# Two layout changes of a fused attention and wave-MLP kernel, moved from TensorE to DMA transposes

## The chip, the core and the metric

The kernel runs on one core of a Trainium2 chip. The core has a matrix engine (TensorE, PE in the profile, with its weight loads shown apart as PEld), VectorE (DVE), ScalarE (ACT), GpSimd (POOL) and SyncE (SP). Matmul results land in PSUM; everything else lives in SBUF, and DMA queues move data between SBUF and device memory. Each engine works through its own list of instructions in order, and so does each DMA queue: a DMA that waits for its data holds back every DMA behind it on the same queue. The metric is the time of one execution on the device in microseconds; lower is better.

## The reference

First comes attention inside chunks of 64 tokens, for 8 batches of 576 tokens with 8 heads of 64. Its result x, with 512 channels per token, goes through one layer of a wave MLP with a residual:

```
scores = scale * q_c @ k_c^T          # per chunk of 64 tokens
x      = softmax(scores) @ v_c        # x: (8, 576, 512)
theta  = x @ w_theta
zr, zi = x * cos(theta), x * sin(theta)
y      = w_tok_r @ zr + w_tok_i @ zi  # mixes the 576 tokens of a batch
u      = x + y
out    = u + relu(u @ w_ch)
```

Inputs and outputs are float32; the kernel works in float16 with float32 sums.

## The kernel before, in words

The batches are taken in four pairs, numbered p = 0 to 3 in the code. A pair has 1152 tokens, that is nine tiles of 128 rows; tile 4 holds the last 64 tokens of the first batch and the first 64 of the second when outputs are written, and the last 64 tokens of both batches when attention is computed. The attention part treats the tiles in five groups: g = 0, 1, 3, 4 with two tiles each and g = 2 with the one mixed tile.

The steps, each a small function, are: a1 (PE transposes of q and k, then two copies out of PSUM), a2 (scores and exp), a3 (times v, then VectorE divides by the row sums and writes x with tokens on partitions), a4 (L341: PE transposes x, eight 128x128 blocks for a group of two tiles and four for the mixed one, and a copy moves the result to xT, channels on partitions), a5 (theta = x @ w_theta from xT, then cos and sin on ScalarE), z (the products; for the mixed tile two small DMAs on SP's queue put halves together in zm), y (L449: 18 matmuls per batch bb and channel block db; VectorE adds xT and writes uT, channels on partitions, at L463; yh is the same for the first batch of pair 0), w (L470) and st (out_tile, L491).

The function w does two things for a tile j of 128 tokens. For each of four channel blocks, uT is the stationary operand of a 512 wide matmul with w_ch (L475), which sums u @ w_ch, and then of a 128 wide matmul with the identity (L482), which puts u itself, tokens on partitions, into the other half of the same PSUM tile. ScalarE takes relu of the first half into SBUF (L488). In out_tile, VectorE adds the u half and the relu (L494), and SP's queue stores the tile (L496), in two DMAs for tile 4.

Nothing is scheduled at run time. The list ORDER is a written-out sequence of these steps (name, pair, group or block, and bits that choose the engine of a copy); the program emits them in this order, so each engine's own order follows from it. All PSUM tiles come from one pool of four buffers, two banks each, taken in turn; a step whose buffer is still being read waits. Of o, the output tile, there are four buffers; x has six, uT and xT two each. Loads of q, k and v with a cast to float16 go through POOL's queue. A DMA on SP's queue also waits for the one issued eight before it.

Of the kernel before, what the change touches and what calls it, by code (L numbers as in the profile page):

```python
# [9 lines left out]
FP32 = mybir.dt.float32  # L10
FP16 = mybir.dt.float16
AF = mybir.ActivationFunctionType
ALU = mybir.AluOpType
# [3 lines left out]


ORDER = """
a1.0.0:0 a2.0.0:0 a1.0.1:3 a3.0.0.0:0 a3.0.0.1:0 a2.0.1:0 a1.0.2:0 a3.0.1.0:0 a2.0.2:0  # L20
a3.0.2.0:0 a4.0.2:3 a4.0.0:0 a3.0.1.1:0 a5.0.2:0 a4.0.1:1 z.0.2.0:0 a5.0.1:0 a5.0.0:0
tw.1.2:0 z.0.0.0:0 z.0.0.1:0 tw.0.0:1 z.0.1.0:0 z.0.1.1:0 tw.1.1:1 tw.0.1:0 tw.0.2:0
tw.1.0:1 a1.0.3:2 yh.0.0:0 a2.0.3:0 yh.0.1:0 a1.0.4:2 a3.0.3.0:0 yh.1.0:0 a3.0.3.1:0
a2.0.4:0 yh.1.1:0 a1.1.0:0 a3.0.4.0:0 a3.0.4.1:0 w.0.0:0 a2.1.0:0 a4.0.3:0 st.0.0:0
a4.0.4:1 a3.1.0.0:0 a1.1.1:0 a3.1.0.1:0 a5.0.3:0 a4.1.0:1 w.0.1:0 st.0.1:0 a5.0.4:0
a1.1.2:2 z.0.3.0:0 a5.1.0:0 w.0.2:0 z.0.4.0:0 z.0.3.1:0 z.0.4.1:0 a2.1.1:0 st.0.2:0
a1.1.3:2 w.0.3:0 st.0.3:0 y.0.1.0:0 a2.1.2:0 a3.1.1.0:0 a1.1.4:1 a3.1.2.0:0 a2.1.3:0
y.0.1.1:0 a1.2.0:0 a3.1.3.0:0 a3.1.1.1:0 y.0.1.2:0 a2.1.4:0 a3.1.3.1:0 z.1.0.0:0
a1.2.1:3 a2.2.0:0 a3.1.4.0:0 y.0.1.3:0 a1.2.2:0 a3.1.4.1:0 a2.2.1:0 a4.1.1:1 z.1.0.1:0
w.0.4:0 st.0.4:0 a4.1.2:0 a4.1.3:0 w.0.5:0 st.0.5:0 a3.2.1.0:0 a1.2.3:2 a5.1.2:0 w.0.6:0  # L30
z.1.2.0:0 a5.1.1:0 st.0.6:0 w.0.7:0 a5.1.3:0 st.0.7:0 z.1.1.0:0 a4.1.4:1 w.0.8:0
st.0.8:0 a1.2.4:1 z.1.1.1:0 a3.2.1.1:0 a5.1.4:0 z.1.3.0:0 z.1.4.0:0 y.1.0.0:0 a2.2.2:0
z.1.4.1:0 a3.2.0.0:0 z.1.3.1:0 a1.3.0:3 y.1.0.1:0 y.1.1.0:0 a2.2.3:0 a3.2.0.1:0 a2.2.4:0
a1.3.1:3 a3.2.3.0:0 y.1.0.2:0 a1.3.2:0 a3.2.2.0:0 a2.3.0:0 a2.3.1:0 a1.3.3:0 a3.2.3.1:0
y.1.0.3:0 a4.2.0:0 a4.2.2:0 a4.2.1:0 y.1.1.1:0 a2.3.2:0 a3.3.0.0:0 a1.3.4:0 a3.2.4.0:0
a2.3.3:0 w.1.0:0 a5.2.2:0 a5.2.0:0 st.1.0:0 z.2.2.0:0 w.1.1:0 a4.2.3:1 a5.2.1:0 st.1.1:0
z.2.0.0:0 z.2.1.0:0 y.1.1.2:0 z.2.0.1:0 a3.2.4.1:0 a3.3.3.0:0 w.1.2:0 a5.2.3:0 st.1.2:0
z.2.1.1:0 y.1.1.3:0 a3.3.0.1:0 a3.3.1.0:0 w.1.3:0 st.1.3:0 y.2.0.0:0 a4.2.4:1 w.1.4:0
a3.3.2.0:0 st.1.4:0 a3.3.3.1:0 z.2.3.0:0 a5.2.4:0 y.2.0.1:0 a4.3.0:0 a4.3.2:1 z.2.3.1:0
w.1.5:0 st.1.5:0 z.2.4.0:0 y.2.0.2:0 a4.3.3:0 w.1.6:0 a2.3.4:0 st.1.6:0 a3.3.1.1:0  # L40
z.2.4.1:0 y.2.0.3:0 w.1.7:0 a4.3.1:1 st.1.7:0 y.2.1.0:0 a3.3.4.0:0 a3.3.4.1:0 a5.3.2:0
a5.3.1:0 z.3.1.0:0 w.1.8:0 a5.3.0:0 st.1.8:0 w.2.0:0 z.3.2.0:0 y.2.1.1:0 st.2.0:0
w.2.1:0 z.3.0.0:0 z.3.0.1:0 st.2.1:0 z.3.1.1:0 a5.3.3:0 y.2.1.2:0 w.2.2:0 a4.3.4:1
st.2.2:0 y.2.1.3:0 w.2.3:0 z.3.3.0:0 st.2.3:0 a5.3.4:0 w.2.4:0 z.3.3.1:0 y.3.0.0:0
w.2.5:0 z.3.4.0:0 st.2.4:0 st.2.5:0 y.3.0.1:0 w.2.6:0 st.2.6:0 y.3.0.2:0 z.3.4.1:0
w.2.7:0 st.2.7:0 y.3.0.3:0 w.2.8:0 y.3.1.0:0 w.3.0:0 st.2.8:0 y.3.1.1:0 w.3.1:0 st.3.0:0
st.3.1:0 y.3.1.2:0 w.3.2:0 st.3.2:0 y.3.1.3:0 w.3.3:0 st.3.3:0 w.3.4:0 st.3.4:0 w.3.5:0
w.3.6:0 st.3.5:0 st.3.6:0 w.3.7:0 st.3.7:0 w.3.8:0 st.3.8:0
""".split()


# [1 line left out]
def kernel(  # L53
# [11 lines left out]
    nc = tc.nc  # L65
    B, H, S, D = q.shape
    DM = H * D
    CH = 64
    P = 128
    NDB = DM // P  # L70
    NE = H // 2
    NP = B // 2
    T = 2 * S
    NT = T // P
    HS = S // 2
    KT = S // P
# [22 lines left out]
    id16 = const.tile([P, P], FP16, name="id16")  # L99
# [131 lines left out]
    st = {}  # L231
# [4 lines left out]
    def once(p, key, make):  # L236
        if key not in st[p]:
            st[p][key] = make()
        return st[p][key]
# [9 lines left out]
    def xT_tile(p):  # L249
        return once(p, "xT", lambda: pairp.tile([P, NDB, T], FP16, name="xT"))  # L250

    def uT_tile(p):
        return once(p, "uT", lambda: pairp.tile([P, NDB, T], FP16, name="uT"))
# [87 lines left out]
    def a4(p, g, bits):  # L341

        j0, n = GROUPS[g]
        ps = psum2("ps_xT", FP16)
        psv = ps[:, 0 : NDB * n * P].rearrange("p (a s) -> p a s", a=NDB)
        for jj in range(n):
            for db in range(NDB):
                nc.tensor.transpose(  # L348
                    psv[:, db, jj * P : jj * P + P],
                    st[p]["x", g][:, jj, db * P : db * P + P],  # L350
                    id16,
                )
        xT = xT_tile(p)
        if n == 2:
            copy(bits & 1, xT[:, :, x_col(j0) : x_col(j0) + n * P], psv)
            return
        xm = trig.tile([P, NDB, P], FP16, name="xTm", bufs=1)
        st[p]["xTm"] = xm
        copy(bits & 1, xm, psv)
        copy(  # L360
            not bits & 2,
            xT.rearrange("p a (b s) -> p a b s", b=2)[:, :, :, KT * P : S],
            xm.rearrange("p a (b s) -> p a b s", b=2),
        )

    def a5(p, g):
# [82 lines left out]
    def y(p, bb, db):  # L449
# [17 lines left out]
            op=ALU.add,  # L467
        )

    def w(p, j):  # L470

        uT = uT_tile(p)
        ps = psum2("ps_uw")
        for db in range(NDB):
            nc.tensor.matmul(  # L475
                ps[:, 0:DM],
                uT[:, db, j * P : j * P + P],
                wch16[:, db, :],
                start=(db == 0),
                stop=(db == NDB - 1),  # L480
            )
            nc.tensor.matmul(  # L482
                ps[:, DM + db * P : DM + db * P + P],
                uT[:, db, j * P : j * P + P],
                id16,
            )
        r = outp.tile([P, DM], FP32, name="relu", bufs=3)
        nc.scalar.activation(out=r, in_=ps[:, 0:DM], func=AF.Relu)  # L488
        st[p]["w", j] = (ps, r)

    def out_tile(p, j):  # L491
        ps, r = st[p].pop(("w", j))
        o = outp.tile([P, DM], FP32, name="o32")
        nc.vector.tensor_tensor(out=o, in0=ps[:, DM : 2 * DM], in1=r, op=ALU.add)  # L494
        for pp, bb, s0, n in out_ranges(j):
            nc.sync.dma_start(out[2 * p + bb, s0 : s0 + n, :], o[pp : pp + n])  # L496


    BATCH = [[0, 1, 2], [3, 4]]
# [2 lines left out]
    def load(i):  # L502
        load_qk(*LOADS[i])
        load_v(*LOADS[i])
# [13 lines left out]
    load_w(moe_w_ch, wch16)  # L518
    for i in range(5, NAT):
        load(i)  # L520
    loaded = NAT
    seen = set()
    emit = dict(a1=a1, a2=a2, a3=a3, a4=a4, a5=a5, z=z, y=y, yh=yh, w=w,
                st=out_tile, tw=tw)
    for item in ORDER:
        name, bits = item.split(":")
        kind, *args = name.split(".")
        args = [int(i) for i in args]
        if kind in ("a1", "a4", "tw"):
            emit[kind](*args, int(bits))  # L530
        else:
            emit[kind](*args)
        seen.add(name)

        while loaded < len(LOADS):
            p, g = LOADS[loaded]
            pn, gn = LOADS[loaded - NAT]
            need = {f"a1.{pn}.{gn}"}
            if p >= 2:
                need |= {f"a3.{p - 2}.{g}.{hg}" for hg in range(GROUPS[g][1])}  # L540
            if not need <= seen:
                break
            load(loaded)
            loaded += 1
# [29 lines left out]
```

The softmax here doesn't subtract the row's maximum and nothing guards it: scores larger than these inputs give would overflow.

## Time and profile before

| what | value |
|---|---|
| median of 11 runs (lowest to highest) | 223.03 us (221.8 to 224.67) |
| the profiled execution's own time | 224.2 us |
| its span from first to last instruction | 222.1 us |
| PE busy | 199.5 us (90%) |
| DVE, ACT, POOL busy | 130.9, 117.4, 85.1 us |
| mean granted TensorE clock | 0.992 |
| chain that ended last, PE's share | 82% |

Busy time of the engines in stretches of the span, from the trace: in 0 to 12 us PE works 3.73 us, in 12 to 35 us 16.98 of 23, in 60 to 85 us 22.29 of 25, in 85 to 110 us 25.00 of 25, in 110 to 135 us 24.49 of 25, and in 135 to 211 us it has no idle time. POOL's DMAs fill the first half of the span; in 110 to 222 us POOL has none. Times in the profile are microseconds, "mean ns" is the duration of one instruction, and because matmuls are pipelined, two matmuls that follow each other are closer together than one's duration.

### The profile page before, as it was taken

To read this page: it belongs to the slowest core of one execution; us is meant where nothing else is said; L and a number is where in the kernel's file an instruction comes from. 1 tells how busy PE (TensorE), PEld (TensorE's weight loads), DVE (VectorE), ACT (ScalarE), POOL (GpSimd) and SP (SyncE) were. 2 spreads that over 40 slices of the span, in tenths; PEclk is the share of its full clock that TensorE was granted. 3 is DMA by queue.
4 is the path that set the end of the run, shared out by engine and by line. 5 is a ranking of instruction groups with operands and counts; after the bars stand their busy time and mean duration, and the time that the engine had idled before them with its cause. 6 is when DMAs were issued, how large, how long until landed. Compare 5 with 4: busy or idle time off the path is not lost.

```text
span 222.1 us, 6717 instructions
## 1 busy us (share of the span) xinstructions
PE 199.5 (90%) x2994; PEld 139.5 (63%) x2994; DVE 130.9 (59%) x230; ACT 117.4 (53%) x136; POOL 85.1 (38%) x118
## 2 busy tenths in 40 slices
PE   0575889989999888999999999999999999999992
PEld 0464458767578665566787755667765676777751
DVE  0145556766585683768765539777665653653553
ACT  2243796046996355699247696416758425221242
POOL 7897488579796598848600000000000000000000
PEclk9999999999999996999999999999999999999999
DMA  6999999999999999999990012112211221321236
GB/s 60 176 125 188 195 183 182 175 151 140 171 198 221 127 143 172 196 205 238 172 77 6 3 47 74 47 50 47 99 47 49 88 79 50 94 94 49 96 117 215
DMA packets 83612, 26.92 MB, mean 121 GB/s; under 512 B 76288, under 2 KB 78976, under 8 KB 83584
## 3 DMA queue, kind: packets, MB, share of 16 engines
q0 software_dynamic: 77696, 16.54, 83.9%
q1 hardware_dynamic: 5888, 9.96, 13.2%
q8 instruction: 23, 0.38, 0.7%
q14 instruction: 5, 0.04, 0.1%
HBM read 33.06 MB, written 9.44 MB: 191 GB/s over the span
## 4 chain that ended last, share of the span: by engine, by line
PE 82%; ACT 7%; DVE 5%; issue 2%; DMA 2%; POOL 0%; ACTq 0%; POOLq 0%
PE ps_y L455 27%; PE ps_uw L475 14%; PE ps_theta L377 14%; PE ps_qkT L266 8%; PE ps_y L434 4%; PE ps_sT L292 4%; PE ps_xT L348 4%; PE ps_uw L482 4%; PE ps_x L320 3%; DMA qk<-in_k_dram 2%; ACT kT L199 2%; ACT eT L299 2%; DVE x L334 1%; DVE kT L197 1%; DVE qT L197 1%
## 5 line engine op out<-in xcount | busy, mean ns | idle before, releaser
L455 PE MATMUL ps_y<-wT,z 128*128 128x288 f16 x448 | 59.5, 286 | 0.0
L455 PEld LDWEIGHTS <-z 128*128 128x128 f16 x448 | 42.6, 98 | 12.9 <-issue 0.3
L176 POOL DMA_DIRECT2D v<-in_v_dram x56 | 42.0, 762 | 18.0 <-DMA qk<-in_k_dram 10.8
L475 PE MATMUL ps_uw<-wch,uT 128*128 128x512 f16 x144 | 43.5, 386 | 0.0
L488 ACT ACTIVATE relu<-ps_uw 128x512 f32<-128x512 f32 x36 | 21.5, 598 | 39.3 <-PE ps_uw L482 39.2
L463 DVE TENSOR_TENSOR uT<-ps_y,xT 128x576 f16<-128x576 f32 x28 | 21.2, 756 | 26.9 <-PE ps_y L455 26.8
L494 DVE TENSOR_TENSOR o<-ps_uw,relu 128x512 f32<-128x512 f32 x36 | 24.7, 689 | 19.2 <-ACT relu L488 19.1
L482 PE MATMUL ps_uw<-id,uT 128*128 128x128 f16 x144 | 31.9, 222 | 0.0
L377 PE MATMUL ps_theta<-wtheta,xT 128*128 128x512 f16 x128 | 30.1, 379 | 0.8 <-DVE xT L197 0.8
L299 ACT ACTIVATE eT<-ps_sT 128x1024 f16<-128x1024 f32 (+1 forms) x20 | 18.6, 940 | 20.7 <-PE ps_sT L292 20.7
L266 PE MATMUL ps_qkT<-id,qk 128*64 128x128 f16 (+1 forms) x640 | 22.3, 226 | 6.9 <-DMA qk<-in_q_dram 5.8
L387 ACT ACTIVATE cos<-ps_theta,pihalf 128x1024 f16<-128x1024 f32 (+1 forms) x20 | 20.6, 1031 | 11.4 <-PE ps_theta L377 11.3
L334 DVE TENSOR_TENSOR x<-ps_x,recip 128x512 f16<-128x512 f32 x36 | 24.9, 692 | 1.2
L266 PEld LDWEIGHTS <-qk 128*64 128x64 f16 (+1 forms) x640 | 19.1, 118 | 9.7 <-DMA qk<-in_q_dram 5.8
L475 PEld LDWEIGHTS <-uT 128*128 128x128 f16 x144 | 14.3, 99 | 15.3 <-issue 0.8
L199 ACT COPY kT<-ps_qkT 128x1024 f16<-128x1024 f16 (+1 forms) x11 | 12.6, 1149 | 20.6 <-DVE qT L197 20.5
L155 POOL DMA_DIRECT2D qk<-in_k_dram x24 | 19.1, 797 | 4.1 <-DMA qk<-in_q_dram 2.7
L377 PEld LDWEIGHTS <-xT 128*128 128x128 f16 x128 | 11.8, 98 | 14.0 <-DVE xT L197 1.0
L155 POOL DMA_DIRECT2D qk<-in_q_dram x24 | 19.3, 805 | 1.9 <-issue 1.0
L391 ACT ACTIVATE sin<-ps_theta 128x1024 f16<-128x1024 f32 (+1 forms) x20 | 18.7, 936 | 0.0
L292 PE MATMUL ps_sT<-qT,kT 64*64 64x64 f16 x576 | 13.0, 224 | 5.7 <-ACT kT L199 3.3
L197 DVE COPY kT<-ps_qkT 128x1024 f16<-128x1024 f16 (+1 forms) x9 | 11.1, 1235 | 7.3 <-ACT qT L199 7.3
(51 smaller groups left out, 207.5 us busy)
## 6 DMA issues: line engine op xcount, KB each, us to landing
out_dram<-o SPq DMA_DIRECT2D x32, 256.0 KB, 2.0
qk<-in_q_dram POOLq DMA_DIRECT2D x16, 256.0 KB, 6.4
qk<-in_k_dram POOLq DMA_DIRECT2D x16, 256.0 KB, 7.6
v<-in_v_dram POOLq DMA_DIRECT2D x40, 64.0 KB, 6.6
v<-in_v_dram POOLq DMA_DIRECT2D x16, 128.0 KB, 6.2
out_dram<-o SPq DMA_DIRECT2D x8, 128.0 KB, 2.4
wnat<-in_moe_w_tok_r_dram POOLq DMA_DIRECT2D x2, 288.0 KB, 8.1
wnat<-in_moe_w_tok_i_dram POOLq DMA_DIRECT2D x2, 288.0 KB, 9.5
```

The costliest lines, as they stand in the source:

```text
L155: nc.gpsimd.dma_start(t[(pp // 2) : (pp // 2) + m // 2, ti].rearrange("p h t d -> p h (t d)"), src.rearrange("h (p t) d -> p h (t d)", t=2),)
L176: nc.gpsimd.dma_start(v16[pp : pp + m, sl, :, 0:D], v[2 * p + bb, :, s0 : s0 + m, :].rearrange("h s d -> s h d"),)
L266: nc.tensor.transpose(psv[par * D : par * D + D, w, e, tk, 0:rows], t[0:rows, w, 2 * e + par, tk, :], id16[0:rows, 0:rows],)
L292: nc.tensor.matmul(psv[kh * CH : kh * CH + CH, par, i, e, :], kT[par * D : par * D + D, e, c0 : c0 + CH], qT[par * D : par * D + D, e, c0 ...
L299: nc.scalar.activation(out=eT[:, 0:n].rearrange("p i e r c -> p r (i e) c"), in_=psv[:, :, 0:n].rearrange("p r i e c -> p r (i e) c"), fun ...
L334: nc.vector.tensor_tensor(out=xo, in0=px[:, :, :, 0:D], in1=recip.broadcast_to((P, 2, NE, D)), op=ALU.mult,)
L377: nc.tensor.matmul(ps[:, jj * DM : jj * DM + DM], xt[:, db, :], wtheta16[:, db, :], start=(db == 0), stop=(db == NDB - 1),)
L455: nc.tensor.matmul(psv[:, hf, 0:HS], zt[:, db * P : db * P + P], wT[:, kt, hf * HS : hf * HS + HS], start=(kt == 0), stop=(kt == 2 * KT),)
L475: nc.tensor.matmul(ps[:, 0:DM], uT[:, db, j * P : j * P + P], wch16[:, db, :], start=(db == 0), stop=(db == NDB - 1),)
L482: nc.tensor.matmul(ps[:, DM + db * P : DM + db * P + P], uT[:, db, j * P : j * P + P], id16,)
L488: nc.scalar.activation(out=r, in_=ps[:, 0:DM], func=AF.Relu)
L494: nc.vector.tensor_tensor(out=o, in0=ps[:, DM : 2 * DM], in1=r, op=ALU.add)
```

## The change

For pair 0, u is still turned by PE and ends as before. For pairs 1 to 3 (U_DMA = 1) the identity matmuls and the relu go away. A new step ut issues a DMA transpose on SP's queue, which turns one channel block of uT, over 512 tokens (bb = 0) or 640 tokens (bb = 1), into the tile un with tokens on partitions: eight DMAs per pair. The end of a tile is then one VectorE instruction, max(u @ w_ch, 0) + u, which reads the matmul's result in PSUM and un in SBUF.

For pairs 2 and 3 (X_DMA = 2) the step a4 goes away. A new step xt turns x into xT by DMA transposes on SP's queue, one per tile of 128 tokens: nine DMAs per pair. The copy that spreads the mixed tile over xT becomes a step of its own, xm. Outputs of pairs 2 and 3 (ST_POOL = 2) are stored through POOL's queue, those of pairs 0 and 1 through SP's as before. ORDER is written anew as a whole.

The lines of the diff, with most of ORDER left out (its parts that matter are quoted in the prediction):

```diff
+    U_DMA = 1
+    X_DMA = 2
+    ST_POOL = 2
...
         copy(bits & 1, xm, psv)
+        xm_copy(p, bits >> 1)
+
+    def xt(p, g):
+        j0, n = GROUPS[g]
+        x = st[p]["x", g]
+        xT = xT_tile(p)
+        if n == 1:
+            xm = trig.tile([P, NDB, P], FP16, name="xTm", bufs=1)
+            st[p]["xTm"] = xm
+            nc.sync.dma_start_transpose(xm, x[:, 0, :])
+            return
+        for jj in range(n):
+            c0 = x_col(j0 + jj)
+            nc.sync.dma_start_transpose(xT[:, :, c0 : c0 + P], x[:, jj, :])
+
+    def xm_copy(p, bits):
         copy(
-            not bits & 2,
-            xT.rearrange("p a (b s) -> p a b s", b=2)[:, :, :, KT * P : S],
-            xm.rearrange("p a (b s) -> p a b s", b=2),
+            not bits & 1,
+            xT_tile(p).rearrange("p a (b s) -> p a b s", b=2)[:, :, :, KT * P : S],
+            st[p]["xTm"].rearrange("p a (b s) -> p a b s", b=2),
         )
...
+    def un_tile(p, bb):
+        return once(p, ("un", bb), lambda: pairp.tile(
+            [P, KT + bb, DM], FP16, name=f"un{bb}", bufs=1))
+
+    def ut(p, bb, db):
+        cols = slice(KT * P, T) if bb else slice(0, KT * P)
+        nc.sync.dma_start_transpose(
+            un_tile(p, bb)[:, :, db * P : db * P + P], uT_tile(p)[:, db, cols]
+        )
+
     def w(p, j):
...
-            nc.tensor.matmul(
-                ps[:, DM + db * P : DM + db * P + P],
-                uT[:, db, j * P : j * P + P],
-                id16,
-            )
-        r = outp.tile([P, DM], FP32, name="relu", bufs=3)
-        nc.scalar.activation(out=r, in_=ps[:, 0:DM], func=AF.Relu)
+            if p < U_DMA:
+                nc.tensor.matmul(
+                    ps[:, DM + db * P : DM + db * P + P],
+                    uT[:, db, j * P : j * P + P],
+                    id16,
+                )
+        r = None
+        if p < U_DMA:
+            r = outp.tile([P, DM], FP32, name="relu", bufs=3)
+            nc.scalar.activation(out=r, in_=ps[:, 0:DM], func=AF.Relu)
         st[p]["w", j] = (ps, r)
...
-        nc.vector.tensor_tensor(out=o, in0=ps[:, DM : 2 * DM], in1=r, op=ALU.add)
+        if p < U_DMA:
+            nc.vector.tensor_tensor(out=o, in0=ps[:, DM : 2 * DM], in1=r, op=ALU.add)
+        else:
+            nc.vector.scalar_tensor_tensor(
+                out=o,
+                in0=ps[:, 0:DM],
+                scalar=0.0,
+                in1=un_tile(p, int(j >= KT))[:, j % KT if j < KT else j - KT],
+                op0=ALU.max,
+                op1=ALU.add,
+            )
+        eng = nc.sync if p < ST_POOL else nc.gpsimd
         for pp, bb, s0, n in out_ranges(j):
-            nc.sync.dma_start(out[2 * p + bb, s0 : s0 + n, :], o[pp : pp + n])
+            eng.dma_start(out[2 * p + bb, s0 : s0 + n, :], o[pp : pp + n])
```

More of the change, by code (lines that the diff above doesn't have):

```diff
@@ L19 @@
 ORDER = """
[L20 to L48, printed above, removed]
+a1.0.0:3 a1.0.1:2 a2.0.0:0 a1.0.2:3 a2.0.2:0 a2.0.1:0 a3.0.0.0:0 a3.0.0.1:0 a3.0.2.0:0
+a3.0.1.0:0 a3.0.1.1:0 a4.0.2:0 a4.0.0:0 a4.0.1:1 a5.0.2:0 z.0.2.0:0 a5.0.0:0 z.0.0.0:0
@@ new lines @@
+a5.0.1:0 tw.1.2:0 tw.0.0:0 tw.1.1:1 z.0.1.0:0 z.0.0.1:0 tw.0.2:1 a1.0.3:0 z.0.1.1:0
+tw.0.1:0 tw.1.0:1 a2.0.3:0 yh.0.0:0 a1.0.4:2 a3.0.3.0:0 yh.0.1:0 a3.0.3.1:0 a2.0.4:0
+yh.1.0:0 a3.0.4.0:0 a1.1.0:3 a3.0.4.1:0 a2.1.0:0 a4.0.3:1 a4.0.4:0 a3.1.0.0:0 a5.0.3:0
+z.0.3.0:0 a3.1.0.1:0 a1.1.1:0 yh.1.1:0 z.0.3.1:0 a5.0.4:0 a1.1.2:2 z.0.4.0:0 z.0.4.1:0
+a2.1.1:0 a1.1.3:2 w.0.0:0 st.0.0:0 y.0.1.0:0 a2.1.2:0 a1.1.4:0 a2.1.3:0 a3.1.1.0:0
+y.0.1.1:0 a4.1.0:0 a3.1.1.1:0 a1.2.0:0 a3.1.2.0:0 a3.1.3.0:0 y.0.1.2:0 a4.1.1:0 a4.1.2:1
@@ new lines @@
+a2.1.4:0 a2.2.0:0 a3.1.3.1:0 w.0.1:0 st.0.1:0 a5.1.2:0 a4.1.3:1 a5.1.1:0 w.0.2:0
+z.1.2.0:0 a5.1.0:0 z.1.1.0:0 st.0.2:0 z.1.1.1:0 z.1.0.0:0 w.0.3:0 z.1.0.1:0 st.0.3:0
+y.0.1.3:0 a3.1.4.0:0 a1.2.1:3 a3.1.4.1:0 w.0.4:0 st.0.4:0 y.1.0.0:0 a4.1.4:1 a5.1.3:0
+a5.1.4:0 z.1.4.0:0 y.1.0.1:0 a3.2.0.0:0 z.1.3.0:0 a1.2.2:1 z.1.4.1:0 ut.1.0.0:0 a2.2.1:0
+a1.2.3:2 w.0.5:0 st.0.5:0 y.1.0.2:0 a2.2.2:0 a1.2.4:1 z.1.3.1:0 a3.2.0.1:0 ut.1.0.1:0
+a3.2.2.0:0 y.1.0.3:0 a3.2.1.0:0 a2.2.4:0 a2.2.3:0 a1.3.0:0 ut.1.0.2:0 xt.2.2:0
@@ new lines @@
+a3.2.4.0:0 a1.3.1:0 y.1.1.0:0 a1.3.2:1 a3.2.1.1:0 xm.2.2:0 xt.2.0:0 ut.1.1.0:0 a2.3.0:0
+y.1.1.1:0 a3.2.4.1:0 a3.2.3.0:0 w.0.6:0 xt.2.1:0 a5.2.2:0 a5.2.0:0 st.0.6:0 w.0.7:0
+z.2.2.0:0 a5.2.1:0 st.0.7:0 z.2.1.0:0 y.1.1.2:0 w.0.8:0 z.2.1.1:0 z.2.0.0:0 st.0.8:0
+ut.1.0.3:0 a3.3.0.0:0 z.2.0.1:0 a2.3.1:0 y.1.1.3:0 a1.3.3:1 a3.3.0.1:0 a3.2.3.1:0
+y.2.0.0:0 a2.3.2:0 xt.2.4:0 a3.3.1.0:0 a1.3.4:0 a3.3.1.1:0 xt.2.3:0 a2.3.3:0 ut.1.1.1:0
+y.2.0.1:0 a3.3.3.0:0 a2.3.4:0 a3.3.2.0:0 ut.1.1.3:0 a5.2.4:0 w.1.0:0 st.1.0:0 xt.3.0:0
@@ new lines @@
+ut.1.1.2:0 y.2.0.2:0 w.1.1:0 st.1.1:0 a5.2.3:0 w.1.2:0 st.1.2:0 xt.3.1:0 z.2.3.0:0
+z.2.3.1:0 a5.3.0:0 z.2.4.0:0 w.1.3:0 st.1.3:0 xt.3.2:0 ut.2.0.1:0 a3.3.4.0:0 y.2.0.3:0
+a3.3.4.1:0 z.2.4.1:0 a3.3.3.1:0 w.1.4:0 a5.3.1:0 w.1.5:0 ut.2.0.2:0 z.3.0.0:0 ut.2.0.3:0
+st.1.4:0 st.1.5:0 z.3.1.0:0 z.3.1.1:0 z.3.0.1:0 xt.3.3:0 y.2.1.0:0 w.1.6:0 xm.3.2:0
+a5.3.2:0 st.1.6:0 xt.3.4:0 y.2.1.1:0 w.1.7:0 z.3.2.0:0 y.2.1.2:0 w.1.8:0 ut.2.0.0:0
+st.1.7:0 y.2.1.3:0 st.1.8:0 w.2.0:0 y.3.0.0:0 st.2.0:0 w.2.1:0 a5.3.4:0 ut.2.1.0:0
@@ new lines @@
+ut.2.1.1:0 w.2.2:0 st.2.1:0 a5.3.3:0 st.2.2:0 ut.2.1.3:0 w.2.3:0 st.2.3:0 y.3.0.1:0
+z.3.4.0:0 z.3.4.1:0 ut.2.1.2:0 z.3.3.0:0 z.3.3.1:0 w.2.4:0 y.3.0.2:0 w.2.5:0 st.2.4:0
+ut.3.0.1:0 ut.3.0.2:0 y.3.0.3:0 st.2.5:0 w.2.6:0 st.2.6:0 y.3.1.0:0 w.2.7:0 st.2.7:0
+y.3.1.1:0 w.2.8:0 ut.3.0.0:0 ut.3.0.3:0 st.2.8:0 y.3.1.2:0 ut.3.1.0:0 w.3.0:0 ut.3.1.1:0
+st.3.0:0 ut.3.1.2:0 y.3.1.3:0 w.3.1:0 w.3.2:0 ut.3.1.3:0 st.3.1:0 st.3.2:0 w.3.3:0
+w.3.4:0 w.3.5:0 st.3.3:0 w.3.6:0 st.3.4:0 w.3.7:0 st.3.5:0 st.3.6:0 st.3.7:0 w.3.8:0
@@ L49 @@
+st.3.8:0
 """.split()
@@ L523 @@
     emit = dict(a1=a1, a2=a2, a3=a3, a4=a4, a5=a5, z=z, y=y, yh=yh, w=w,
-                st=out_tile, tw=tw)
+                st=out_tile, tw=tw, xt=xt, xm=lambda p, g, bits: xm_copy(p, bits), ut=ut)
     for item in ORDER:
@@ L528 @@
         args = [int(i) for i in args]
-        if kind in ("a1", "a4", "tw"):
+        if kind in ("a1", "a4", "tw", "xm"):
             emit[kind](*args, int(bits))
```

## The prediction

> **What bounds the kernel now.** I read the page's busy times first, then the slices of the span, then the chain that ended last.
>
> ```profile
> PE 199.5 (90%) x2994; PEld 139.5 (63%) x2994; DVE 130.9 (59%) x230; ACT 117.4 (53%) x136; POOL 85.1 (38%) x118
> ...
> PE   0575889989999888999999999999999999999992
> ...
> POOL 7897488579796598848600000000000000000000
> PEclk9999999999999996999999999999999999999999
> DMA  6999999999999999999990012112211221321236
> ...
> q0 software_dynamic: 77696, 16.54, 83.9%
> q1 hardware_dynamic: 5888, 9.96, 13.2%
> ...
> PE 82%; ACT 7%; DVE 5%; issue 2%; DMA 2%; POOL 0%; ACTq 0%; POOLq 0%
> ...
> L475 PE MATMUL ps_uw<-wch,uT 128*128 128x512 f16 x144 | 43.5, 386 | 0.0
> L488 ACT ACTIVATE relu<-ps_uw 128x512 f32<-128x512 f32 x36 | 21.5, 598 | 39.3 <-PE ps_uw L482 39.2
> ...
> L494 DVE TENSOR_TENSOR o<-ps_uw,relu 128x512 f32<-128x512 f32 x36 | 24.7, 689 | 19.2 <-ACT relu L488 19.1
> L482 PE MATMUL ps_uw<-id,uT 128*128 128x128 f16 x144 | 31.9, 222 | 0.0
> ...
> out_dram<-o SPq DMA_DIRECT2D x32, 256.0 KB, 2.0
> ...
> zm<-zmid SPq DMA_DIRECT2D x8, 64.0 KB, 3.9
> ```
>
> From about 85 us on PE has no gap, while loads and POOL end at half the span. VectorE and ScalarE wait for PE (39.2 and 19.1 us of relu and o idle are waits down PE's own output). So in the second half a PE microsecond is a real one, and the DMA engines are nearly free. All removed PE work lies there.
>
> What one matmul costs in the stream is read not from "mean ns" but from the chain in order of time:
>
> ```profile
> 86.12 0.43 PE ps_uw L475
> ...
> 145.83 0.45 PE ps_xT L348 x8
> ...
> 208.80 0.22 PE ps_uw L475
> 209.02 0.06 PE ps_uw L482
> 209.07 2.21 PE ps_y L455 x18
> 211.28 0.21 PE ps_uw L475
> ```
>
> From one 512 wide matmul to the next are 0.27 us, of which the identity matmul has 0.055. Eight x transposes take 0.45 us, 0.056 each. At 211.28 the last y is done; the span's last 10.8 us are the tail: uT's add, six tiles of w, relu, o, store.
>
> **The change part by part.**
>
> *PE.* Identity matmuls: 27 tiles x 4 x 0.055 = 5.9 us. Transposes of x: 2 pairs x 36 x 0.056 = 4.0 us. What counts is the end of the last y. Ahead of it go 4.0 us of x transposes and 19 tiles x 0.22 = 4.2 us (pair 1, pair 2, one tile of pair 3); and the new order has one w of pair 3 ahead of the last y where the old has three, which moves 2 x 1.09 = 2.2 us behind it. Sum **-10.4 us**.
>
> *ScalarE and VectorE.* 27 relus of 0.598 (16.1 us) go; so do ten copies of xT and xTm (0.69 on VectorE, 1.01 on ScalarE). The new end instruction reads PSUM and SBUF as L494 does; the trace has no row of it. Bounds: 0.42 (a 64-row product of 512) and 0.689 + 0.598, the two it replaces; I take 0.69, L494's. All lies beside PE: nothing, as long as PE is the bound. If not, ScalarE still has 16 us less.
>
> *The transposes.* 42 DMAs come onto SP's queue: 18 for x and 12 for u of 128 KB, 12 for u of 160 KB; some 20 stores leave it for POOL. The trace has no transpose. Cheapest price: the hardware queue's own rate, 9.96 MB in 13.2% of 222.1 us, so 0.39 us for 128 KB. Dearest: if pieces of 64 bytes count like the software queue's packets (83.9% x 222.1 x 16 / 77696 = 38.4 ns on one engine), 2048 / 16 x 38.4 = 4.9 us. I take pieces of 256 bytes, a row of one 128 block, since those loads average 213 bytes a packet: 512 / 16 x 38.4 ns = **1.23 us** for 128 KB, 1.54 for 160. Landing after that: 2.0 us as the stores; zm's 3.9 is the other end, partly under the loads. With these prices the queue works 30 x 1.23 + 12 x 1.54 = 55 us plus about 11 for zm and stores, in some 110 us.
>
> *A wait.* SP's queue is in order, and stores now stand before transposes. The tightest place: the store of tile 1.0 waits for its o, behind it stand both transposes of xt.3.0, and PE needs them at a5.3.0. From the end of w.1.0 PE has y 2.21, w 0.87, a5 1.73, w 0.87 = 5.7 us; the path is o 0.69, store issue 0.34, 2 x 1.23, landing 2.0, with 0.1 of hand-overs 5.6. An o that finds VectorE inside another 0.69 operation is late by that: **+0.6**. At a5.3.1 PE has 6.5 us for the same path.
>
> *The tail.* After the last y: uT add 0.76; transpose 1.54 + 2.0; o of tile 4 0.69, at 5.0. Its two stores are on POOL, 0.77 each (POOL's rows for loads) where SP's take 0.34. The fifth o needs the buffer of tile 4, whose stores have landed at 5.0 + 1.54 + 2.0 to 3.1 (POOL's fastest landing seen for a load) = 8.5 to 9.6; then 0.69, 0.77, landing, and the 0.6 us close of now: 12.6 to 14.8, I take 13.7 against 10.8, **+2.9**.
>
> *The start.* The new order puts two groups' q, k transposes before the first scores and takes group 2 before group 1. Group 2's q and k land near 12.0 us (issued 7.2, median landing 4.8), then come 32 transposes 0.6, drain 0.2, copies 0.59 and 0.73, and both groups' scores 0.37 and 0.62: the first a3 has its turn near 15.1 us, where it now starts with the landing of v at 14.1. By 28 us both orders meet the landing of the token weights (issue 17.7 and 18.4, landing 9.5). I take **+1.0**; bounds -3 (the 1.8 us stall at 82.4 and the half clock behind it, shown by the 0.43 us line above, do not come back) and +3.
>
> Sum: -10.4 + 0.6 + 2.9 + 1.0 = -5.9; span 222.1 to 216.2. The profiled execution took 224.2, 1.2 over the median of 223.03; the median stands 0.9 over this span. So **217.1 us**.
>
> [...]
>
> **The rivals.**
>
> *SP's queue becomes the bound (slower).* From the end of w.0.8 to z.3.2 PE has 37.3 us of work, and SP must issue 20 transposes (20.75 units of 128 KB), eight stores (2.7 us) and two zm (1.1). It keeps up to 33.5 / 20.75 = 1.6 us per unit. Beyond, each 0.1 us costs 2.1 us in this stretch alone, up to 4.5 if no later slack takes it up (45 units in all). At 2.0 us: +8 to +18 on 217.1, so 225 to 235; at 2.5 at least 236. The 5.9 us gained are gone 0.13 to 0.28 us past 1.6, near 1.8. For it: a transpose must cut rows up, and 256 byte pieces are my choice; smaller ones reach the point at once. Against: SP is idle now, and the DMA share is one to three tenths.
>
> *Landing is late, not the queue.* With zm's 3.9 instead of 2.0, a5.3.0 is late by 1.9, a5.3.1 by 1.2, the tail by 1.9: +5, about 222. For it: the median of the only small SBUF to SBUF move; against: half of those fell into the loads.
>
> *Transfers are hidden anyway.* At 0.39 us the tail shortens by 1 and the 0.6 goes; with the start's gain of 3 instead of its loss, 217.1 - 5 = about 212; without, 215.5.
>
> **How the numbers follow.** Chances: forecast 0.45 (own range 214.5 to 220.5, the bounds of start and tail), hidden 0.12, late landing 0.10, queue bound 0.33 (half of it under 232). Half a per cent, 1.1 us, is what this measurement can tell. Late landing lies on the line: 0.03 of it faster, 0.04 same, 0.03 slower. Faster gets 0.45 + 0.12 + 0.03, less 0.02 for the forecast's upper end, 0.58; same 0.04 and 0.03 from both sides, 0.07; slower 0.35. The range 213.5 to 232 leaves out about 0.03 below and 0.16 above.
>
> **What would show it.** PE's group L482 has 36 matmuls instead of 144 and the x transposes 72; from 110 us PE's slices stay at 9. If the queue bounds, PE's waits name xT (a5.2, a5.3) or zm of pair 3, SP's queue waits for no one, and the clock falls in stalls as at 86 us. Transposes longer than 1.6 us apart on SP would make me wrong; so would a tail over 15 us, or the first 85 us changed by over 3.

## The result, and the profile after

| | before | after |
|---|---|---|
| median (lowest to highest) | 223.15 us (221.51 to 228.11, 47 executions) | 220.32 us (218.68 to 222.75, 12 executions) |
| ratio, after to before | | 0.9867, 95% interval 0.9835 to 0.9899 |
| profiled execution: its time, its span | 224.2, 222.1 us | 220.16, 218.0 us |
| end of the last y | 211.28 us | 204.36 us |
| from there to the end of the span | 10.8 us | 13.6 us |

The change makes the kernel 1.3% faster, about half of the 2.7% forecast; 220.32 lies inside the range given. Where a kernel's own executions spread by more than 1.5% (u alone, and the change's second run after2, below), its ratio is made from its lowest few, and I use the median of all there.

The page of the changed kernel, busy times, slices, queues, shares of the chain, and two groups:

```profile
PE 191.5 (88%) x2814; PEld 130.1 (60%) x2814; DVE 126.9 (58%) x223; ACT 98.8 (45%) x106; POOL 96.0 (44%) x138
...
PE   0666978969999999999957999999999999999970
...
PEclk9999999997999999999988999999999999999997
DMA  5999999999999999999999923463668568283883
...
q1 hardware_dynamic: 27648, 11.15, 26.9%
q8 instruction: 22, 0.36, 0.7%
...
PE 72%; DMA 12%; POOL 4%; issue 4%; ACT 4%; DVE 2%; POOLq 0%; DVEq 0%; ACTq 0%
...
L537 DVE SCALAR_TENSOR_TENSOR o<-ps_uw,un 128x512 f32<-128x512 f32 x27 | 18.3, 688 | 9.5 <-PE ps_uw L512 7.0
```

PE has lost 180 matmuls and is still the engine that sets the pace. Three things are new: the slices 57 in PE's row near 109 to 120 us, where it had nines; clock digits below 9 at 49 to 55 us and at 109 to 120 us, where before had a single 6, at 83 to 89 us; and "issue" with 4% of the chain, where before it had 2%. The end instruction takes 688 ns, VectorE and ScalarE stay far from their limits.

The transposes themselves, from the views of the tiles un and xT (columns: shortest/median/longest ns of one on SP's queue, first and last start in us), and from the list of DMA issues (last column: median us from issue to landing):

```profile
L503 SPq DMA_TRANSPOSE un<-uT x24: 1189/1272/2635, 91.8 to 205.2; - x24
```

```profile
L383 SPq DMA_TRANSPOSE xT<-x x16: 1200/1257/2277, 107.6 to 170.2; - x16
```

```profile
un<-uT SPq DMA_TRANSPOSE x24, 3.0
xT<-x SPq DMA_TRANSPOSE x16, 3.1
xTm<-x SPq DMA_TRANSPOSE x2, 6.4
```

So a transpose holds the queue for 1.26 us, and lands 3.0 us after the beginning of its issue, that is about 1.5 us after it lets go of the queue. The two mixed tiles, one of them issued among the last loads, have a median of 6.4; the six transposes issued between 91 and 111 us, while loads still ran, took 8.0 to 11.2 us to land.

Where the time up to the last y went is read by stages. The rows below are the windows of the two kernels, before first; the columns are window, width, then busy us (count) of PE, PE's weight loads, VectorE, ScalarE and POOL, then granted clock, DMA share (packets that overlap are each counted, so it can pass 1) and GB/s.

```profile
0.00:12.00 12.00, 3.73 (x82) 3.17 (x84) 0.87 (x3) 3.41 (x3) 10.12 (x19) 1.00 1.29 121
40.00:62.00 22.00, 21.26 (x400) 13.86 (x398) 15.01 (x28) 12.88 (x14) 16.53 (x23) 1.00 1.79 158
62.00:100.00 38.00, 35.28 (x708) 25.32 (x700) 25.59 (x45) 24.51 (x29) 28.30 (x39) 0.96 1.83 181
100.00:135.00 35.00, 34.49 (x667) 25.40 (x666) 22.36 (x41) 24.56 (x28) 8.53 (x11) 1.00 0.77 90
```

```profile
0.00:12.00 12.00, 4.86 (x102) 3.97 (x104) 2.04 (x4) 2.30 (x2) 10.36 (x20) 1.00 1.30 121
40.00:62.00 22.00, 19.64 (x386) 13.41 (x384) 13.88 (x27) 11.81 (x11) 17.19 (x25) 0.92 1.87 154
62.00:100.00 38.00, 38.00 (x655) 27.12 (x653) 26.95 (x49) 25.64 (x31) 27.57 (x38) 1.00 1.87 182
100.00:135.00 35.00, 30.72 (x549) 21.47 (x548) 19.97 (x38) 20.80 (x24) 8.59 (x11) 0.95 1.28 113
```

Width less PE's busy time is its idle time: 8.27, 0.74, 2.72 and 0.51 us before, 7.14, 2.36, 0.00 and 4.28 after (12 to 40 us is alike, 6.0 in both, and from 135 us to the last y there is none): 18.3 against 19.8 us, +1.5. The other loss is half clock, a stretch in which the clock records of the trace have the granted clock at 0.5: a matmul of L475 took 0.43 us of the chain of before in it (at 86.12 us) and 0.22 outside (at 208.80). Up to the last y there is one such stretch of 3.41 us before (from 85.5 us) and there are two after (from 48.4 and 113.2 us); PE has no idle time in them, so I put the cost of each at half its length, 1.7 us, and the difference at +1.7. The windows show them as 0.96, 0.92 and 0.95. The stops of 62 to 100 us have gone; in the chain of before they were

```profile
72.86 0.90 issue
...
82.44 1.81 issue
```

New ones have come ahead of them and behind them. The end of the last y moved by -6.9 us, from 211.28 to 204.36; without the +1.5 and the +1.7 that is -10.1 us for the matmuls that went.

The chain of the changed kernel in order of time shows the new stalls:

```profile
47.50 0.69 PE ps_sT L301 x32
...
50.18 2.65 PE ps_theta L403 x8
...
107.67 0.95 PE ps_qkT L275 x29
108.62 3.12 issue
111.74 0.30 PE ps_qkT L275 x3
...
113.30 3.96 PE ps_y L481 x18
...
118.01 0.18 PE ps_sT L301 x6
118.19 1.16 issue
119.35 0.56 PE ps_sT L301 x23
```

PE stops for 3.12 us in the middle of the 32 transposes of one step, waiting for nothing that the profile shows, and the y behind it takes 3.96 us instead of 2.21. It stops again at 118 us. The stall at 45 us is another: PE waits 2.18 us for kT (k transposed, which the scores need), and then runs eight theta matmuls in 2.65 us instead of 1.73. In the list of waits (total us, times, longest) it is the longer of these two:

```profile
PE ps_sT L301 <- DVE kT L206: 3.7, 2, 2.2
```

### The profile page after: what moved, and what is told of

Same layout as the page of the kernel before. It is cut to its first block, busy times and chain, and to the rows that moved or that the text cites. A ratio compares the mean times of both kernels' runs of the same rounds, so it can differ in the third digit from the quotient of the medians.

```text
span 218.0 us, 6379 instructions
## 1 busy us (share of the span) xinstructions
PE 191.5 (88%) x2814; PEld 130.1 (60%) x2814; DVE 126.9 (58%) x223; ACT 98.8 (45%) x106; POOL 96.0 (44%) x138
## 4 chain that ended last, share of the span: by engine, by line
PE 72%; DMA 12%; POOL 4%; issue 4%; ACT 4%; DVE 2%; POOLq 0%; DVEq 0%; ACTq 0%
PE ps_y L481 30%; PE ps_theta L403 12%; PE ps_uw L512 12%; DMA qk<-in_k_dram 7%; PE ps_qkT L275 6%; PE ps_sT L301 4%; DMA wtheta<-in_moe_w_theta_dram 3%; PE ps_y L460 3%; PE ps_x L329 3%; PE ps_xT L357 2%; POOL v L185 2%; DMA un<-uT 1%; ACT kT L208 1%; POOL out_dram L547 1%; POOL qk L164 1%
## 5 line engine op out<-in xcount | busy, mean ns | idle before, releaser
L481 PE MATMUL ps_y<-wT,z 128*128 128x288 f16 x448 | 61.2, 291 | 0.0
L481 PEld LDWEIGHTS <-z 128*128 128x128 f16 x448 | 43.7, 100 | 15.2
L547 POOL DMA_DIRECT2D out_dram<-o x20 | 10.9, 546 | 90.0 <-DVE o L537 90.0
L512 PE MATMUL ps_uw<-wch,uT 128*128 128x512 f16 x144 | 37.4, 379 | 0.2 <-ACT sin L417 0.2
L403 PE MATMUL ps_theta<-wtheta,xT 128*128 128x512 f16 x128 | 31.2, 391 | 0.0
L537 DVE SCALAR_TENSOR_TENSOR o<-ps_uw,un 128x512 f32<-128x512 f32 x27 | 18.3, 688 | 9.5 <-PE ps_uw L512 7.0
L403 PEld LDWEIGHTS <-xT 128*128 128x128 f16 x128 | 12.6, 101 | 15.2 <-issue 2.2
L208 ACT COPY kT<-ps_qkT 128x1024 f16<-128x1024 f16 (+1 forms) x11 | 13.3, 1205 | 10.5 <-DVE qT L206 10.3
L428 DVE TENSOR_TENSOR z<-x,cos 128x1024 f16<-128x1024 f16 x16 | 11.0, 686 | 8.9 <-ACT cos L413 8.9
L206 DVE COPY kT<-ps_qkT 128x1024 f16<-128x1024 f16 (+1 forms) x9 | 10.5, 1172 | 9.5 <-ACT qT L208 9.5
```

What stands on the lines that cost most here:

```text
L403: nc.tensor.matmul(ps[:, jj * DM : jj * DM + DM], xt[:, db, :], wtheta16[:, db, :], start=(db == 0), stop=(db == NDB - 1),)
L481: nc.tensor.matmul(psv[:, hf, 0:HS], zt[:, db * P : db * P + P], wT[:, kt, hf * HS : hf * HS + HS], start=(kt == 0), stop=(kt == 2 * KT),)
L512: nc.tensor.matmul(ps[:, 0:DM], uT[:, db, j * P : j * P + P], wch16[:, db, :], start=(db == 0), stop=(db == NDB - 1),)
```

## The experiments

The theory after the result was: the transposes cost what was forecast, but the first ones run beside the last cast loads of POOL's queue, where PE's next instructions come late. The rivals: the new order itself loses the time; SP's queue is near its limit; the stores on POOL lose it in the tail.

**The parts alone.** Three kernels keep the new order and take out parts: order_alone has neither u nor x by DMA and all stores on SP; u_alone and x_alone have one of the two.

```diff
-    U_DMA = 1          # order_alone, x_alone: 4
-    X_DMA = 2          # order_alone, u_alone: 4
-    ST_POOL = 2        # order_alone: 4
 # ORDER: each xt.p.g becomes a4.p.g where x stays on PE (xm dropped); ut dropped where u stays
```

> The new ORDER with all the old operations: identity matmuls and relu for every pair, x turned by PE at the places of xt, all stores on SP's queue. PE has the work of before. Theory 'instruction stalls' (the shortfall of the change, some 3 us, comes from PE waiting for its own instructions behind loads and first transposes, and from the half clock after it): with no transposes on the queues the order alone costs 0 to 1 us, 223 to 224 us. Rival 'order' (the new sequence itself loses the 3 us in its first half): 226 to 227 us, with PE idle in the first 85 us 3 us longer than before.

> The change without the x part: u of pairs 1 to 3 by DMA transpose (24 DMAs), x of all pairs turned by PE at the places of xt. By the terms of the prediction: 4.2 + 2.2 us less ahead of the last y, tail +2.9, start +1.0, so -2.5, about 220.5 us. Theory 'instruction stalls': three transposes remain beside the loads, and a stall over 1 us between 100 and 120 us remains with them. Rival 'order': 222 to 224 us without such a stall.

> The change without the u part: x of pairs 2 and 3 by DMA transpose (18 DMAs), u by identity matmuls and relu in every pair, stores as in the change. By the terms: -4.0, start +1.0, wait up to +0.6, so -2.4 to -3.0, about 220.5 us; the last part after the last y stays PE's, eight tiles of 1.09 us and relu, o and store. If the DMA transposes were late for theta, PE's waits would name xT at a5.3.0: theory says not (the two take 1.27 us each and land 3.1 after issue), none over 0.5 us.

| kernel | median us | ratio to before, interval | last y | from there to the end |
|---|---|---|---|---|
| order_alone | 225.15 | 1.0031 (0.9988 to 1.0073) | 207.9 | 13.0 |
| order_alone2, same kernel, measured beside order_dummy | 225.02 | 1.0093 (1.0058 to 1.0128) | 210.8 | 13.0 |
| u_alone | 223.51 of 10; before beside it 223.88 | by medians 0.998; 0.9896 (0.9824 to 0.9968) from its lowest three | 207.8 | 13.6 |
| x_alone | 225.99 | 1.0103 (1.0062 to 1.0144) | 208.5 | 15.0 |
| the change | 220.32 | 0.9867 (0.9835 to 0.9899) | 204.4 | 13.6 |

None of the three came out as expected. order_alone is 1.3 us over the before beside it and order_alone2 2.7 us, between the theory and the rival; u_alone is 3.0 us and x_alone 5.5 us slower than the terms gave. u_alone does have the stop that the theory wanted, 3.02 us behind the 29th transpose of q and k, and x_alone one of 2.39 us. The profile of order_alone happens to show its fastest execution (222.69); that of order_alone2 (225.53) is near its median. The new order without a transpose is no gain: it has the stall at 45 us with the half clock behind it (0.92 in 40 to 62 us), and a tail 2.2 us longer than before, the two w that now stand behind the last y. u alone shows no certain gain (by medians 0.2%), and x alone is a loss: its last y is 2.3 us earlier than in order_alone2, not 4.0, and the tail is 2.0 longer: the last o ends 10.05 us after the last y in both, so the difference lies behind it, where the last store goes through POOL. Only together do they pay: 6.4 us less up to the last y, for 8.2 us of PE's work.

**The first transposes beside the loads.** late moves three transposes of u behind the loads and leaves three tiles of x on PE, so that six transposes fewer stand between 92 and 115 us. PE gets 0.7 us of work back (12 blocks).

```diff
-... z.1.4.1:0 ut.1.0.0:0 a2.2.1:0 ... ut.1.0.1:0 ... ut.1.0.2:0 xt.2.2:0 ... xm.2.2:0 xt.2.0:0 ... ut.1.0.3:0
+... z.1.4.1:0 a2.2.1:0 ... a4.2.2:0 ... a4.2.0:0 ... ut.1.0.0:0 ut.1.0.1:0 ut.1.0.2:0 ut.1.0.3:0
```

> The change with no transpose beside the loads: the first three of u of pair 1 move behind w.0.8, next to the fourth, and x of groups 0 and 2 of pair 2 goes back to PE (0.67 us of transposes). Theory 'instruction stalls' with the transposes as their cause: the two gaps of the changed kernel at 108.6 (3.1 us) and 118.2 (1.2 us) and the half clock behind the first (1.75 us) shrink to what before shows there (0 to 1 us): 4 us less, plus 0.7, about 217 us. Rival 'loads alone make PE's instructions late': gaps of 1 to 3 us stay where PE crosses into new instructions while loads run, about 220 to 221 us.

217.61 us, ratio 0.9736 (0.9675 to 0.9798). It was run twice more, each time beside the change on the same chip:

> The changed kernel again, beside the three others of this group: ratio to before 0.987, and in a second profile again gaps without a cause of 2 to 3 us at 108 us and about 1 us at 118 us, if they belong to the program and not to one execution.

> The kernel without transposes beside the loads again: ratio 0.974, 1.3% under the changed kernel. The profile of its relative with another tail showed a gap of 2.05 us at 108 us although no transpose was under way, where this one had shown 0.94. Theory 'transposes make the instructions late': 1 us or less again here. Rival 'the loads do it, more or less by chance': 1 to 3 us, and the difference to the changed kernel has another source (the second gap, the transposes' own waits).

> The changed kernel once more, beside the two others of this group. So far 0.987 and 0.977 of before in two groups; PE's idle time from 100 to 135 us was 4.3 and 5.3 us in its two profiles.

> The kernel without transposes beside the loads once more. So far 0.974 and 0.972; PE idle from 100 to 135 us 2.0 and 2.2 us. Theory 'transposes beside loads cost PE its instructions': idle 2 to 2.5 us again against 3.3 to 5.3 for the changed kernel, and a time 2 to 3 us under it. Rival 'chance': the two overlap in idle time and in time.

The change had 219.96 and 219.77 us, late 217.30 and 217.73: 2.7 and 2.0 us less. By the ratios to before the gain is smaller and the intervals overlap: 0.9768 (0.969 to 0.9846) against 0.9723 (0.967 to 0.9776), and 0.9827 (0.9767 to 0.9886) against 0.9781 (0.9749 to 0.9813). But late is ahead in all three pairs of medians by 2 us or more, and of the 72 pairings of single executions within the last two pairs in 55, although PE does more work in it. The windows of the last pair, the change first:

```profile
100.00:135.00 35.00, 31.66 (x551) 22.26 (x549) 20.18 (x39) 20.89 (x25) 9.38 (x12) 0.90 1.33 114
```

```profile
100.00:135.00 35.00, 33.80 (x644) 24.49 (x643) 23.12 (x44) 24.56 (x29) 9.38 (x12) 1.00 0.91 109
```

PE is idle for 3.34 us in one and 1.20 in the other, and the half clock (0.90, so 3.4 us) is gone. In the six profiles that have all transposes in their places PE is idle for 3.3 to 7.5 us in this window (7.5 with every transpose doubled), in the five profiles of late and its two successors 1.2 to 2.4, in those of the order without transposes 1.1 and 2.6. The stops that the profile gives no cause for ("issue") make up 3.3 to 5.3 us of it in the first group, 0 to 2.1 in the second, 0 and 1.5 in the third.

**Whose gap it is.** shift puts 20 small transposes of the identity into a spare PSUM tile ahead of PE's first work. Nothing reads them. A gap that belongs to a place in the work stays behind the 29th transpose of q and k; one that belongs to a place in PE's list moves 20 matmuls forward.

```diff
+    pad = psum2("ps_pad", FP16)
+    for _ in range(20):
+        nc.tensor.transpose(pad[0:CH, 0:CH], id16[0:CH, 0:CH], id16[0:CH, 0:CH])
```

> The change with 20 small transposes of the identity put ahead of PE's first instruction, while PE waits for the first load. PE's list has weight loads and matmuls as separate instructions; in both traces the gaps without a cause stand at instruction 175 of a block of 256 (before 2735, changed 3503 and 3759, counted in PE's own list). Forty more instructions in front shift every block by 40. Theory 'instruction stalls' (PE waits for the next 256 instructions to be fetched): the gap at about 108 us comes 20 pairs earlier in a1.3.0, behind its 9th transpose and not behind its 29th, and the second behind the 7th matmul of a3.2.1.1 or not at all. Rival 'a hidden wait of that instruction': it stays behind the 29th. Time within 1 us of the changed kernel.

One execution, 219.65 us. PE's timeline (start, duration, instruction, count; in brackets the idle time before it):

```profile
108.29 0.47 PE L275 MATMUL ps_qkT<-id,qk 128*64 128x128 f16 x9
111.06 0.86 PE L275 MATMUL ps_qkT<-id,qk 128*64 128x128 f16 x23 [2.30 <-issue]
...
118.80 0.29 PE L329 MATMUL ps_x<-v,eT 64*64 64x65 f16 x11 [1.02 <-issue]
```

The gap moved from behind the 29th to behind the 9th, by exactly 20; the second one moved ahead into the products with v as well, behind 5 of them and not 7 as I had counted. Counted by the matmuls and weight loads that the trace shows as begun, PE stops in the changed kernel behind 3503 and 3755 of them, before the change behind 2226 and 2735 (the expectation's 3759 is 4 too high): 252 apart after, 509 before and 768 from the second of before to the first of after, all four the 171st to 178th of a block of 256. The row q8 of the page fits such blocks: 22 packets of 16 KB bring instructions, one for 256 of PE's 5628 matmuls and weight loads; before it is 23 packets, one for 260 of 5988. And the trace has the time of each packet: after each of the 24 such stops of over 0.3 us between 60 and 206 us, in all profiles, PE goes on 1.2 to 2.1 us after one of them has been read (1.40 and 1.71 us in the two of before, 2.07 and 1.39 in the two after). No view names what PE waits for there; from the place that moved and these times I take it to be its own instructions.

**Six transposes that nothing needs.** order_dummy is order_alone with six transposes into a spare tile at the places of those that late had moved.

```diff
+    def du(p, db):
+        nc.sync.dma_start_transpose(spare(), uT_tile(p)[:, db, 0 : KT * P])
+    def dx(p, g):
+        for jj in range(GROUPS[g][1]):
+            nc.sync.dma_start_transpose(spare(), st[p]["x", g][:, jj, :])
 # ORDER: du.1.0 du.1.1 du.1.2 dx.2.2 dx.2.0 at the places of ut.1.0.0-2, xt.2.2, xt.2.0
```

> The new ORDER with all the old operations, and beside them six DMA transposes that nothing reads, at the places of ut.1.0.0 to 2, xt.2.2 and xt.2.0: three of uT and three of x go into a spare tile while the loads still run. PE's list is that of the order alone. Theory 'transposes make the instructions late': gaps of 2 to 4 us at 108 to 120 us and the half clock behind them, 3 to 5 us more than the order alone, ratio to before 1.017 to 1.025. Rival: as the order alone, ratio 1.003.

> The new ORDER with all the old operations again, as the base of the kernel with six transposes added: ratio 1.003, no gap over 0.5 us at 108 to 120 us by the theory 'transposes make the instructions late'; one of 1 to 3 us at 108 us if the loads alone do it by chance.

227.56 us, ratio 1.0216 (1.0172 to 1.026), against 1.0093 for the order alone measured beside it. Six transposes that no instruction waits for cost 2.5 us: this work on the queue was not free, though nothing needed its result. The windows of the two, order_dummy first:

```profile
100.00:135.00 35.00, 32.88 (x577) 23.50 (x575) 21.01 (x39) 23.94 (x28) 8.28 (x11) 0.95 1.03 104
```

```profile
100.00:135.00 35.00, 32.42 (x638) 23.57 (x637) 21.38 (x41) 23.72 (x28) 8.11 (x11) 1.00 0.73 85
```

PE's idle time is no larger (2.12 and 2.58 us): the stop behind the 29th is longer, 2.07 us against 1.50, but two waits for kT of 0.6 and 0.5 us are gone. The loss shows as half clock behind the longer stop (0.95, 1.7 us: the next 32 transposes of q and k take 1.85 us instead of 1.01, y 2.60 instead of 2.31), and the last y ends 1.7 us later.

**How late the instructions come.** The packet that ends the second stop of the changed kernel is the 14th of the instruction queue. From the moment when PE begins entry 3455 of the same count until the reading of this packet begins, 9.0 us pass in the changed kernel (107.73 to 116.69) and 6.8 to 9.3 in the six profiles with all transposes in their places, 8.2 and 8.4 in u_alone and x_alone, and 7.4 in order_dummy; in the five of late and its successors 5.0 to 5.6, in those of the order alone 4.5 and 5.8. So with transposes beside the loads, idle ones too, this packet came later. For the 13th packet, which ends the first stop, the same count (from entry 3199; 5.2 us in the changed kernel) overlaps: 3.3 to 5.6 us with transposes beside the loads, 2.0 to 4.6 without.

**The queue's limit.** double issues every transpose twice, the second into a spare tile.

```diff
...
             nc.sync.dma_start_transpose(xT[:, :, c0 : c0 + P], x[:, jj, :])
+            nc.sync.dma_start_transpose(spare()[:, 0:NDB, :], x[:, jj, :])
...
+        nc.sync.dma_start_transpose(spare()[:, 0 : KT + bb, :], uT_tile(p)[:, db, cols])
...
```

> The change with every DMA transpose issued twice, the second into a spare tile that nothing reads: 84 transposes on SP's queue, 2.5 us per unit of 128 KB instead of 1.27. Theory 'the queue has a limit' (1.6 us per unit in the stretch from w.0.8 to z.3.2): at least 236 us, PE waiting for xT at a5.3.0 and for zm of pair 3, and SP's queue waiting for nothing. Rival 'the queue is not near its limit': under 226 us.

One execution, 256.19 us. The waits (total us, times, longest):

```profile
DVE o L543 <- DMA un<-uT: 12.0, 4, 8.5
...
PE ps_theta L405 <- DMA xT<-x: 10.6, 7, 5.1
PE ps_y L483 <- DMA zm<-zmid: 10.3, 1, 10.3
```

These are the waits that the rival of the prediction named, xT at a5.3 and zm of pair 3. At 2.5 us for each useful transpose the queue is the bound; at 1.26 it is not. In the changed kernel PE waits for no transposed xT at all.

**The tail.** stores_sp gives all stores back to SP's queue.

```diff
-    ST_POOL = 2
+    ST_POOL = 4
```

> The change with the stores of all pairs on SP's queue. In the changed kernel's trace the last store is issued by POOL at 213.4 us and the span ends at 218.0, 4.6 us later; before, SP's last store took 2.9 us from o to the end. Theory 'the store's queue makes the tail': 1.5 to 2 us less than the changed kernel, about 218.5 us. Rival 'SP's order': stores that wait for o hold up the transposes of pair 3 behind them, and PE or VectorE waits for un: no gain, 220 to 224 us.

219.18 us, ratio 0.9838 (0.9763 to 0.9913): within the interval of the change. The tail is 12.3 us instead of 13.6, but the profiled execution had stops of 1.26 and 3.71 us near 109 and 115 us, and the gain doesn't show.

late_tail takes late, gives o a fifth buffer and SP the last six stores; late_yh also moves yh.1.1 ahead of a2.1.0, so that PE has work while kT is copied at 45 us.

```diff
-        o = outp.tile([P, DM], FP32, name="o32")
+        o = outp.tile([P, DM], FP32, name="o32", bufs=5)
-        eng = nc.sync if p < ST_POOL else nc.gpsimd
+        eng = nc.sync if p < ST_POOL or (p == NP - 1 and j >= 3) else nc.gpsimd
 # late_yh also
-yh.1.0:0 a3.0.4.0:0 a1.1.0:3 a3.0.4.1:0 a2.1.0:0 ... a1.1.1:0 yh.1.1:0 z.0.3.1:0
+yh.1.0:0 a3.0.4.0:0 a1.1.0:3 a3.0.4.1:0 yh.1.1:0 a2.1.0:0 ... a1.1.1:0 z.0.3.1:0
```

> The kernel without transposes beside the loads (217.6 us here, ratio 0.974), with five buffers for o instead of four and the stores of pair 3's tiles 3 to 8 on SP's queue. The tail's terms in the changed kernel's trace: 1.1 us of waiting for o's buffer and 4.6 instead of 2.9 us from the last store to the end: 2.5 us less, about 215 us, ratio 0.963. Rival 'the last transposes bound the tail': SP's transposes of pair 3 are queued in front of these stores, and no more than 1 us is gained.

> The kernel without transposes beside the loads and with the shorter tail (0.971), and one more move: the last of the four yh steps (2.55 us of matmuls) comes ahead of a2.1.0, where every kernel of the new ORDER has PE idle for 2.2 us at 45 us (waiting for kT) and the clock at half for about 3.5 us after it. Theory 'the start is the order's own loss': 2.2 us of idle go, and the 1.75 us of the half clock with them, 3 to 4 us less, ratio 0.955 to 0.96. Rival 'the loads set the pace until 110 us': PE reaches the same later waits for q and k sooner and nothing is gained, ratio 0.968 to 0.974.

late_tail: 216.48 us, 0.9714 (0.9639 to 0.9788), less than I had expected of it. Its tail is 11.5 us against 13.6, but its profile has a stop of 2.05 us at 108.6. late_yh: 215.23 us, 0.9684 (0.9646 to 0.9722), the best of all, 3.2% under the kernel before and 4.5 us under the change measured beside it. The end of its chain:

```profile
199.93 2.21 PE ps_y L480 x18
202.14 6.92 PE ps_uw L511 x32
209.06 0.02 issue
209.08 0.69 DVE o L536
```

In the tail nothing is left but eight tiles of w and the last o and its store. The move of yh.1.1 did not do what it was for: the wait at 45 us is gone, and one of 1.94 us for the next kT stands at 55 us, with the same idle time (2.4) and clock (0.92) in 40 to 62 us as before the move. So late_yh came out as its rival had it (0.968 to 0.974), and the intervals of late_tail and late_yh overlap.

## Why the prediction was half right

*PE, -10.4 us: right within 0.3.* When idle time and clock are set apart, 10.1 us are left for the matmuls that went up to the last y.

*The transposes, 1.23 us and landing 2.0: right for the queue, a little long for the landing.* 1.26 us was measured, 104 GB/s for 128 KB, and 1.28 for 160 KB (I had 1.54). The pieces are there as I took them: 23040 packets of 256 bytes on SP's queue in the trace of after, 512 for 128 KB; but they take 28 ns in the mean, not 38.4. The list counts landing from the beginning of the issue, 3.0 us here, of which the queue has 1.26; about 1.5 us come behind it. I had taken 2.0 and 3.9 from the same list and added them behind the issue, which counted the issue twice.

*The wait at a5.3.0, +0.6: did not come.* PE has no idle time there. In late, which has three more transposes ahead of this step on SP's queue behind w.0.8, it does come: 0.5 and 0.3 us at a5.3.0.

*The end instruction, 0.69: right*, 688 ns.

*The tail, 13.7: right in its sum* (13.6), by luck, since two errors cancel. The o of tile 4 ends at 4.4 us after the last y, not 5.0, and the last o at 8.75, where I had 9.2 to 10.3 (a store takes POOL 0.54 us, not 0.77). But the end comes 4.9 us after the last o, 4.6 after the beginning of its store at 213.40, where I had 3.4 to 4.5. Before, on SP, it came 2.9 us after the last o.

*The start, +1.0: the term that failed.* It stood for all that the new order does to the first 110 us, with the stall at 82 us as the only one known; and what the transposes do to PE while they run beside the last loads stood nowhere in the sum, so it was put at nothing. The stops at 73 and 82 us did go, with the half clock behind them (2.7 and 1.7 us). But PE got 1.6 us of idle time and 1.7 of half clock at 45 to 52 us, which order_alone has too, so that the order brings them; and 3.8 and 1.7 behind 108 us, where I take it to wait for its instructions beside loads and transposes. 1.1 us were won in the first 12. The sum is about +3.2 where the start and the a5.3.0 wait had +1.6. Half clock was in the bounds as a loss that would end, and not as one that could come with a new stall.

*The step to the median: the other half of the miss.* The -5.9 was summed against an execution of 224.2 us and then taken from a median of 223.03. The executions of before that were measured beside the later kernels and took 222.4 to 223.9 us have a granted clock of 0.996 to 1.0, against 0.992 in the one profiled: its half clock behind 82 us is not in most of them, so a change that removes it wins nothing there. In the changed kernel the clock is lower in every one of the 12 executions (0.969 to 0.988). The miss of 3.2 us is 1.8 in the span (-4.1 for -5.9) and 1.4 in this step: the median stands 2.3 us over the profiled span, not 0.9.

*The rivals.* The queue as bound was refuted for this kernel and confirmed as a limit by double. Late landing was refuted, hidden transfers too: the stalls behind 108 us are a loss to what runs beside the transposes, and not to waiting for them. That was in no rival.

What the runs leave open: how much of the first stop belongs to the loads alone (at the same instruction the order without transposes has up to 1.5 us of it, and late_tail, with none beside the loads, 2.05), and by which way a transpose holds up an instruction packet.

## What to carry to other kernels

Price a transfer that is moved to an idle queue by what it does to its neighbours too: here six transposes that nothing waited for cost 2.5 us beside cast loads, and taking six of 42 out from beside them, three to later and three back to PE, won 2.0 to 2.7 by the medians. Look at the clock of many executions before taking a difference from one profile: a stall that only the profiled execution has is no gain to be had. And try parts of a change alone, but do not add them up: here x alone lost 1.0%, u alone gave nothing certain, and the two together won 1.3%.

## What the runs showed of the hardware that I had not expected

- PE stops where no view names anything that it waits for; I take it to run out of instructions. The four stops that were counted (0.90 and 1.81 us before, 3.12 and 1.16 after) stand at nearly the same entry of a block of 256 in its list (509 entries apart before, 252 after), 40 entries added at the front (20 matmuls and their weight loads) moved the first of the changed kernel by 40, and each ends 1.4 to 2.1 us after an instruction packet of 16 KB has been read.
- Half clock came behind longer stops, in stretches of 3.41 us by the clock records of before and after. In the 3.41 us ahead of such a stretch PE was idle for 1.81 us before (the w behind it takes 0.43 instead of 0.22 us) and for 2.18 us (the wait for kT) and 1.94 (of the stop of 3.12) after. In the windows of 100 to 135 us the clock is 0.95 where the longest stop is 2.05 us (late_tail), 2.07 (order_dummy) or 2.30 (shift), and 1.00 where it is 0.94 (late) or 1.50 (order_alone2). The length of a stop doesn't decide it alone: the wait for kT, 2.18 us again in the second profile of the change (after2), left the clock at 1.00 in 40 to 62 us. What else does, no run shows.
- A 160 KB transpose takes no longer on the queue than one of 128 KB (medians 1.28 and 1.26 us).
